# Two layer norms whose later tiles are split in SBUF and transposed by DMA, with a new order of all jobs

## The chip, the core and the metric

The kernel runs on one core of a Trainium2 chip. The time is the device time of one execution in microseconds; the kernel before took 765.34 us as the median of three runs (764.74 to 767.15). Five engines work side by side, each through its own list of instructions in order: TensorE (PE) for matmuls, VectorE (DVE), ScalarE (ACT), GpSimd (POOL) and SyncE (SP), which here does nothing but issue DMA transfers. Matmuls write to PSUM; ACT and DVE carry the results from there to SBUF.

## The reference

Input `x` has 2048 tokens of 512 features. It is normalised, and the result feeds two branches whose sum is added to `x`. (In the sum of the last line `_A_ref` ends with `@ wo`, and `_B_ref` normalises its input a second time.)

```
xn = _layernorm(x)
# A: attention over N = 4 segments of L = 512 tokens, H = 32 heads of 16, with a memory M, z of earlier segments
logits = einsum("bhqd,bhkd->bhqk", qs, ks) * scale + mask
a_dot  = einsum("bhqk,bhkd->bhqd", softmax(logits), vs)
a_mem  = einsum(phi(qs), M) / (einsum(phi(qs), z) + 1e-6)
o = g * a_mem + (1 - g) * a_dot;   M += phi(ks)^T vs;   z += sum phi(ks)
# B: channel MLP, 512 -> 1792 -> 512
y = _layernorm(xn);   h = gelu(y @ w1 + b1);   mlp = h @ w2 + b2
out = x + o @ wo + mlp
```

## The kernel before

**Tiling.** A token tile is 128 tokens by 512 features. The attention runs in 16 units, one for each of four segments and four groups of eight heads; the MLP runs in 16 units, one for each stretch of 256 tokens and each half of the 1792 hidden features. Matrix products are made of float16 parts: an operand is split in a high part and a low part (value times a scale, minus the high part), and a product is three matmuls (`split3`, line 459). So the normalised tokens have to lie in SBUF with features on the partitions, both parts: `xnT` holds a segment for the attention, `yT` 256 tokens for the MLP. There is one buffer of each, so a new segment may be written only when the last reader of the old one is done.

**The norms.** A token tile is loaded into `xt` (two buffers, line 424), its statistics are made on DVE, and POOL applies scale and shift in place (line 412). Then `ln_tr` makes four 128 by 128 transposes on PE into one PSUM tile (line 444), ACT copies the high part out (447) and DVE the low part (448). Of the first norm ("X") there are 16 tiles, of the second ("Y", which loads `x` anew) another 16.

**The jobs.** The work is cut into some 1400 jobs, sorted into streams. In the text: T(i) is a projection of queries or keys of unit i (12 matmuls of 512 columns, line 459), after which ACT and DVE split the result into `hl`, three DMAs write it to DRAM (`qd`, `kd`) and Tr(i) reads it back as stacked rows (`qst`, `kst`, line 500); V is the same for values; M(i) is the pass for row maxima (scores on PE, line 584; masked maximum on DVE, 591); R(i) transposes the maxima (599), which go through DRAM (`md`) into `qst`; S(i) is the scores again (626) with the exponential on ACT (631) and the causal mask on POOL (640); pv and PV multiply by the values (655); O(i) is the chain that divides by the sums (DVE, ACT and POOL, lines 679 to 691); `out` is the output projection of a token tile (782). In the MLP, D is one hidden tile (12 matmuls of 256 columns), G the GELU, H its split, e three matmuls of the second layer (763).

**The order.** Nothing decides the order while the kernel runs: `ORDER` is a string with one letter for each job, a letter names the stream that gives its next job, and each engine gets its instructions in that order, with semaphores in between. SP's list is in the same order, so a DMA that has to wait holds up all DMAs behind it. PSUM has seven rotating tiles for everything but the second MLP layer.

Of the kernel before, what the change touches and what calls it, by code (L numbers as in the profile page):

```python
# [19 lines left out]
P = 128  # L20
D = 512
KT = D // P
# [4 lines left out]
DH = 16  # L27
GH = 8
# [76 lines left out]


ORDER = (
    "aacavveeacccccvccaccvavwwwaawbwwacexxwwwwdfcbyyycxcwwziybxxwygbyxicyzyhyqqzyqqxyqAzAjjjzucqgzqjujrpjrjAzcjAzjf"
    "srpsjjjzssrbzipsujAxikBrcBpssoAjsBsABjAlAqAssljlquljqljAlsqjjCmAmmmjqhjblsjllsqlljqojlBbrBmmcmmjbakBfBqBqriqnq"
    "rginllhqsallsnugllqojjjmmCmBBmqsBljslljlrrujjjjflssljsarjjmiumimmsCsrssjasrnhsrskCnqasssjlqnjllsaaqlllsqqjjmmm"  # L110
    "umarjqjlslsjlaqljsasljsbljsCjjCbfsmmmmrbjssrnokbCgCssqrqinollqqllilqqljsnsjrjjmmmmqjrlsjlsshljlsjlsqjlsjjjmmmm"
    "rofpjinropnkgnipllltulltlujjsprjjjmmmmosjljsjltblujjslblotjjlsmrmmmsjhnskrnssfsqloqsilulqlollsgqinqqmmmmbollos"
    "sjlsljusljshsljbjmmmuramrjqunjqrnfqjqrsijjsoqnjjsrsssoqjskgsqqslallsssaslilsolrrjqjjjummjmmharjssjlqjarssljlaj"
    "ljrssljqsjlaqksmsmammnoqnssaqslsalblsbofnllioolbgbmmmmbhiqllqqllqjlqjlqjromrmmmjnjrnfppjjjsopjjjspsjorsojnrksb"
    "ightslllitllsqljsosjjjmmmmjtljsuusuljlusslljtljjsrmrmmmnjjqrnqqqjkfssroqrsiqllsnollsgillsquosbmmmmbsslosjllsjs"
    "lsjlsljhrujarjmmmmjnjqrnqfuisqsjssrjjorjqqssonjksgssoasslllsssllqqilrajjqrjjqqjarmmmmjjsarljssrssjljslsalllaqj"
    "sasusmmmmnqjqnqhjskassoanbsofllblolillgbimmmmobollflqljlqljqjjrmmmmrnjjrqqpnbjjjsrspsjjosspjoqnjkigtrsslllpoli"
    "ltljssbjjjmmmmqjlsljssljlssljtjrjtjrlmmjqusjmrmnsrnkfqssllsqouqurqqulolliluusgoqsnmmmmibsllsbssllsjlsjqjlursjm"
    "mmmqrnjrjnfjqqrssjisjjoqssrjjqoqsjsrkgssisrsnqrqllolssqsqljrlsjrjsssjlsjmmjjmmqljqljslljljjqlsjkrummmmssnrnssl"
    "llssslllnossmmmmrllllsllorsrmmmmnsssssnnssssstttt"  # L120
)


# [14 lines left out]
def infini_mixer_kernel(ctx: ExitStack, tc: tile.TileContext, x, wq, wk, wv, wo, beta, w1, b1, w2, b2, out):  # L138
    nc = tc.nc
    V, A, G, T, Q = nc.vector, nc.scalar, nc.gpsimd, nc.tensor, nc.sync  # L140
# [3 lines left out]
    cst = ctx.enter_context(tc.tile_pool(name="cst", bufs=1))  # L144
# [295 lines left out]

    def ln_tr(t, dst, c0):
        p = dense()
        for k in range(KT):
            T.transpose(p[:, P * k:P * k + P], t[:, P * k:P * k + P], ident)  # L444
        p3 = p.rearrange("p (k c) -> p k c", k=KT)
        h = dst[:, :, 0, c0:c0 + P]
        A.activation(h, p3, AF.Copy, scale=1024.0)
        V.scalar_tensor_tensor(dst[:, :, 1, c0:c0 + P], p3, 1024.0, h, op0=OP.mult, op1=OP.subtract)  # L448
# [377 lines left out]
    def e_of(j, a, f):  # L826
# [8 lines left out]
        "Y": lambda *k: ln("Y", *k), "Yt": lambda *k: ln_out("Y", *k), "gate": gates,  # L835
# [39 lines left out]
```

## Time and profile before

| | |
|---|---|
| median of three runs | 765.34 us (764.74 to 767.15) |
| the profiled execution | 765.62 us, span 763.9 us |
| PE busy | 721.7 us, 94% of the span |
| DVE, ACT, POOL busy | 550.1, 528.4, 352.9 us |
| mean granted PE clock | 0.984 of full speed |
| transposes of line 444 on `xt` | 120 matmuls |
| DMA issues on SP's queue | none of them a transpose |

The span runs from the first to the last instruction. Busy times are unions of intervals; matmuls overlap in PE's pipeline, so what a piece of work costs PE is read from the distance between starts. "L444" is line 444 of the kernel before. After an arrow in brackets stands what ended an engine's idle time.

### The profile page before, as it was taken

The numbers are of one execution on the slowest core, as the hardware profiler recorded it, in microseconds if no ns is written. First come the engines' busy times: TensorE is split into PE (matmuls) and PEld (weight loads), VectorE is DVE, ScalarE is ACT, GpSimd is POOL, SyncE is SP. The second block draws the span as 40 slices with busy tenths as digits, with TensorE's granted clock in tenths as the row PEclk, the third lists the DMA queues.
The fourth block names the chain that finished last, engine by engine and source line by source line (L and its number), as shares of the span: only waits on it lengthen the run. The fifth ranks groups of instructions, "written<-read, shape, count | busy, mean of one in ns | idle before, by whom it ended". The sixth has DMA issues, their size and how long they took to land.

```text
span 763.9 us, 14514 instructions
## 1 busy us (share of the span) xinstructions
PE 721.7 (94%) x5189; PEld 377.6 (49%) x5189; DVE 550.1 (72%) x1677; ACT 528.4 (69%) x908; POOL 352.9 (46%) x544
## 2 busy tenths in 40 slices
PE   2689999999999999999999999999999999999987
PEld 1354565455643455555454455455555445455433
DVE  5599878998685846888567684979758574777622
ACT  5887898878785478485783577768585567756960
POOL 4466645754624443453434163536335235345461
PEclk9599999999999999999999999999999999999989
DMA  7975314321203223120311324221240315211101
GB/s 206 300 197 146 91 42 107 83 51 51 63 22 113 75 68 103 44 67 23 106 36 36 99 59 125 37 77 30 55 121 1 92 43 108 59 45 42 17 1 56
DMA packets 54084, 59.16 MB, mean 77 GB/s; under 512 B 5038, under 2 KB 40892, under 8 KB 54012
## 3 DMA queue, kind: packets, MB, share of 16 engines
q1 hardware_dynamic: 51708, 54.04, 24.9%
q0 software_dynamic: 2304, 4.20, 3.6%
q8 instruction: 41, 0.67, 0.4%
q14 instruction: 31, 0.25, 0.1%
HBM read 41.18 MB, written 17.04 MB: 76 GB/s over the span
## 4 chain that ended last, share of the span: by engine, by line
PE 77%; ACT 7%; DVE 6%; DMA 5%; issue 2%; SPq 1%; POOL 1%; DVEq 0%; ACTq 0%; POOLq 0%
PE dense L459 31%; PE eacc L763 17%; PE dense L655 8%; PE dense L782 6%; PE dense L584 5%; PE dense L626 5%; ACT pt L631 2%; PE dense L532 2%; PE dense L540 1%; PE dense L560 1%; PE dense L444 1%; DVE dense L591 1%; DMA qst<-qd 1%; DMA qd<-hl 1%; ACT hT L727 1%
## 5 line engine op out<-in xcount | busy, mean ns | idle before, releaser
L591 DVE CUSTOM_DVE_ANT_0 dense<-dense,mask 128x512 f32<-128x512 f32 (+3 forms) x512 | 241.2, 515 | 21.4 <-PE dense L584 14.0
L631 ACT ACTIVATE pt<-dense,qkcs 128x512 f32<-128x512 f32 (+1 forms) x384 | 205.4, 627 | 32.1 <-PE dense L626 31.8
L763 PE MATMUL eacc<-w2s,hT 128*128 128x512 f16 x672 | 171.0, 382 | 1.0 <-DVE acc L767 1.0
L640 POOL TENSOR_SCALAR_AFFINE_SELECT pt<-pt 128x256 f32<-128x256 f32 x256 | 100.9, 426 | 141.1 <-ACT pt L631 140.5
L459 PE MATMUL dense<-yT,w1s 128*128 128x256 f16 x1344 | 161.4, 273 | 3.8 <-DVE yT L448 3.1
L459 PEld LDWEIGHTS <-w1s 128*128 128x128 f16 x1344 | 127.9, 98 | 37.7 <-issue 18.0
L736 POOL TENSOR_TENSOR hT<-hh,hT 128x512 f16<-128x512 f32 x64 | 68.8, 1074 | 88.6 <-ACT hT L735 88.6
L763 PEld LDWEIGHTS <-hT 128*128 128x128 f16 x672 | 58.7, 98 | 77.3 <-issue 27.2
L655 PE MATMUL dense<-pt,vt 128*32 128x512 f32 (+3 forms) x1024 | 79.9, 441 | 0.2
L591 DVE DVE_READ_ACCUMULATOR2_ANT mc<- 128x1 f32 x512 | 72.2, 141 | 0.0
L584 PE MATMUL dense<-kst,qst 48*128 48x512 f16 (+3 forms) x512 | 63.2, 300 | 5.0 <-DVE phk L492 2.2
L735 ACT ACTIVATE hT<-hh 128x512 f16<-128x512 f32 x64 | 36.6, 572 | 43.1 <-POOL hh L734 42.8
L626 PE MATMUL dense<-qst,kst 50*128 50x512 f16 (+3 forms) x512 | 61.7, 300 | 3.5 <-ACT pt L631 1.4
L734 POOL TENSOR_SCALAR hh<-hT,sc 128x512 f32<-128x512 f32 x64 | 42.7, 667 | 40.7 <-ACT hT L727 38.5
L481 DVE SCALAR_TENSOR_TENSOR hl<-dense,hl 128x512 f16<-128x512 f32 x32 | 22.0, 688 | 52.4 <-ACT phq L480 40.1
L655 PEld LDWEIGHTS dense<-pt,vt 128*32 128x32 f32 x1024 | 32.7, 110 | 46.6 <-issue 32.5
L720 ACT ACTIVATE hT<-dense,b1t,sc 128x256 f32<-128x256 f32 x64 | 36.0, 564 | 20.8 <-PE dense L459 20.1
L459 PE MATMUL dense<-xnT,wks 128*128 128x512 f16 x192 | 46.4, 394 | 0.0
L459 PE MATMUL dense<-xnT,wqs 128*128 128x512 f16 x192 | 45.7, 389 | 0.1
L459 PE MATMUL dense<-wvs,xnT 128*128 128x512 f16 x192 | 43.9, 379 | 0.0
L782 PE MATMUL dense<-wos,oT 128*128 128x512 f16 x192 | 43.7, 380 | 0.0
L626 PEld LDWEIGHTS <-kst 50*128 50x128 f16 x512 | 21.0, 94 | 43.8 <-issue 36.0
(223 smaller groups left out, 951.4 us busy)
## 6 DMA issues: line engine op xcount, KB each, us to landing
xt<-in_A_x_dram SPq DMA_DIRECT2D x30, 256.0 KB
kd<-hl SPq DMA_DIRECT2D x48, 128.0 KB
kst<-kd SPq DMA_DIRECT2D x32, 192.0 KB
qd<-hl SPq DMA_DIRECT2D x48, 128.0 KB
qst<-qd SPq DMA_DIRECT2D x32, 192.0 KB
acc<-in_A_x_dram SPq DMA_DIRECT2D x16, 256.0 KB
acc<-in_B_b_dram POOLq DMA_DIRECT2D x16, 256.0 KB, 4.5
out_dram<-acc SPq DMA_DIRECT2D x16, 256.0 KB
```

What stands on the lines that cost most here:

```text
L459: T.matmul(p, wsl(ws, k, a), xsl(xs, k, b), start=s0 and i == 0, stop=s1 and i == 3 * n - 1)
L584: T.matmul(p[:, o:o + n], stk[i, 0][r, t, P * qb:P * qb + P], stk[i, 1][r, t, :n], start=True, stop=True)
L591: V.tensor_tensor_reduce(p[:, o:o + n], p[:, o:o + n], mask[:, 512 - n:], 1.0, -3e38, OP.add, OP.max, mc[i][:, 4 * b + t, qb:qb + 1])
L626: T.matmul(p[:, o:o + n], stk[i, 1][r, t, P * kb:P * kb + P], stk[i, 0][r, t, P * kb:], start=True, stop=True)
L631: A.activation(e[:, OFF[kbs[0]]:OFF[kbs[0]] + o], p[:, :o], AF.Exp, scale=qkcs[:, 1, i % NG:i % NG + 1])
L640: G.affine_select(v, v, pattern=[[0, 2], [1, P]], compare_op=OP.is_ge, fill=0.0, base=0, channel_multiplier=-1)
L655: T.matmul(p[32 * c:32 * c + 32, P * kb:], vt[s, kb][:, 4 * g + c, 16 * odd:16 * odd + 32], pt[i, 2 * c + odd][:, OFF[kb]:OFF[kb] + LEN[kb ...
L734: G.tensor_scalar(t, hz[:, z, :], col(SHH + j % 2), 0.0, op0=OP.mult, op1=OP.add)
L735: A.activation(hT[:, z, 0, :], t, AF.Copy)
L736: G.tensor_tensor(hT[:, z, 1, :], t, hT[:, z, 0, :], op=OP.subtract)
L763: T.matmul(p, t[:, u, P * a:P * a + P], w2s[:, fo, v, :], start=fi == 0 and n == 0, stop=fi == FH - 1 and n == 2)
L782: T.matmul(p, o[:, u, P * b:P * b + P], wos[:, g, v, :], start=i == 0, stop=i == 3 * NG - 1)
```

## The change

For all tiles but those of the first norm's first segment and the second norm's first 256 tokens (26 of 32 tiles), the high and low parts are made in SBUF before the transposition: ACT writes the high part to a new tile `xh` (for the second tile of a pair: to the upper half of the first tile's buffer), DVE writes the low part over the lower half of the tile itself. A separate job ("Xq", "Yq") then sends both parts through a DMA transpose into `xnT` or `yT`: two DMAs of 128 KB for each tile, 52 in all, on SP's queue. The constant `bd` becomes bfloat16 (0 and 1 only). The string `ORDER` is new as a whole.

```diff
@@ streams
-            norm += [("X", n, b, k) for k in range(3)] * (n > 0) + [("Xt", n, b, k) for k in range(2)]
+            norm += [("X", n, b, k) for k in range(3)] * (n > 0) + [(m, n, b, k) for m in ("Xt", "Xq")[:1 + (n > 0)] for k in range(2)]
     for n in range(2 * NSEG):
-        again += [("Y", n, 0, 0), ("Y", n, 0, 2), ("Yt", n, 0, 0), ("Yt", n, 0, 1)]
+        again += [("Y", n, 0, 0), ("Y", n, 0, 2), ("Yt", n, 0, 0), ("Yt", n, 0, 1)] + [("Yq", n, 0, k) for k in range(2)] * (n > 0)
@@ ORDER
-    "llssslllnossmmmmrllllsllorsrmmmmnsssssnnssssstttt"
+    "sssljsrsssljjssssrjljsslsljjslsjkmmmmnnsslllllslnsommmmllllloslmmmmnnntttt"
@@ infini_mixer_kernel
-    bd = cst.tile([P, GH, DH], F32, name="bd")
+    bd = cst.tile([P, GH, DH], BF, name="bd")
...
-    def ln_out(kind, n, b, k):
+    def ln_to(kind, n, b, k):
+
         if kind == "X":
             if n not in xnT:
                 xnT[n] = sb.tile([P, KT, 2, SEG], F16, name="xnT")
-            ln_tr(lt["X", n, b][k], xnT[n], 256 * b + P * k)
+            return xnT[n], 256 * b + P * k
+        if n not in yT:
+            yT[n] = sb.tile([P, KT, 2, 256], F16, name="yT")
+        return yT[n], P * k
+
+    def ln_out(kind, n, b, k):
+        if n == 0:
+            ln_tr(lt[kind, n, b][k], *ln_to(kind, n, b, k))
         else:
-            if n not in yT:
-                yT[n] = sb.tile([P, KT, 2, 256], F16, name="yT")
-            ln_tr(lt["Y", n, b][k], yT[n], P * k)
+            ln_parts(kind, n, b, k)
+
+    lp = {}
+
+    def ln_parts(kind, n, b, k):
+        ts = lt[kind, n, b]
+        t = ts[k]
+        h = sb.tile([P, D], F16, name="xh") if k == 0 else ts[0].bitcast(F16)[:, D:]
+        l = t.bitcast(F16)[:, :D]
+        A.activation(h, t, AF.Copy, scale=1024.0)
+        V.scalar_tensor_tensor(l, t, 1024.0, h, op0=OP.mult, op1=OP.subtract)
+        lp[kind, n, b, k] = h, l
+
+    def ln_send(kind, n, b, k):
+        dst, c0 = ln_to(kind, n, b, k)
+        for a, r in enumerate(lp[kind, n, b, k]):
+            Q.dma_start(dst[:, :, a, c0:c0 + P], r, transpose=True)
```

The order moves much. Two places matter for the text. The first is SP's list around the last pair of tiles of the third segment (`xnT` is about to be read by T of unit 8). In the kernel before:

```order
L604 DMA md_101<-mhl 32x2x128
L609 DMA qst_93<-md_101 2x2048 x2
L424 DMA xt<-in_A_x_dram 128x512 x2
L482 DMA kd_96<-hl 8x16x512
L483 DMA kd_96<-hl 8x16x512
L484 DMA kd_96<-hl 8x16x512
L500 DMA kst_94<-kd_96 48x4x512 x2
```

and in the changed one:

```order
L628 DMA md_101<-mhl 32x2x128
L633 DMA qst_93<-md_101 2x2048 x2
L463 DMA_TRANSPOSE xnT<-xh 128x4x128
L463 DMA_TRANSPOSE xnT<-xt 128x4x128 x3
L424 DMA xt<-in_A_x_dram 128x512 x2
L463 DMA_TRANSPOSE yT<-xh 128x4x128
L463 DMA_TRANSPOSE yT<-xt 128x4x128 x3
L506 DMA kd_96<-hl 8x16x512
L507 DMA kd_96<-hl 8x16x512
L508 DMA kd_96<-hl 8x16x512
```

Four transposes of `xnT` now stand ahead of the loads of the second norm's tiles (which reuse the buffers that the transposes read), and four of `yT` ahead of the writes of unit 8's keys.

The second place is the end of DVE's list, where `acc<-eacc` closes a token tile's half of the second MLP layer (seven e jobs on PE come before each) and `mhl<-dense` belongs to R(15), the last transpose of row maxima. Before (R(15)'s row stands five rows above the first):

```order
L517 SCALAR_TENSOR_TENSOR oT<-oT,nD 128x512
L767 SCALAR_TENSOR_TENSOR acc<-eacc,sc,acc 128x512
L516 TENSOR_TENSOR rc<-rc,ame 128x512
L517 SCALAR_TENSOR_TENSOR rc<-rc,ame 128x512
L541 SCALAR_TENSOR_TENSOR ame<-dense,bg,rc 128x512
L668 SCALAR_TENSOR_TENSOR nN<-dense,bg,nN 128x512
L669 SCALAR_TENSOR_TENSOR nD<-dense,eo,nD 128x512
L679 STREAM_SHUFFLE oT<-nD 128x512
L767 SCALAR_TENSOR_TENSOR acc<-eacc,sc,acc 128x512
L516 TENSOR_TENSOR oT<-oT,nD 128x512
L517 SCALAR_TENSOR_TENSOR oT<-oT,nD 128x512
L767 SCALAR_TENSOR_TENSOR acc<-eacc,sc,acc 128x512
```

Changed (R(15)'s row again five rows above the first):

```order
L541 SCALAR_TENSOR_TENSOR oT<-oT,nD 128x512
L540 TENSOR_TENSOR rc<-rc,ame 128x512
L541 SCALAR_TENSOR_TENSOR rc<-rc,ame 128x512
L565 SCALAR_TENSOR_TENSOR ame<-dense,bg,rc 128x512
L791 SCALAR_TENSOR_TENSOR acc<-eacc,sc,acc 128x512
L692 SCALAR_TENSOR_TENSOR nN<-dense,bg,nN 128x512
L693 SCALAR_TENSOR_TENSOR nD<-dense,eo,nD 128x512
L703 STREAM_SHUFFLE oT<-nD 128x512
L540 TENSOR_TENSOR oT<-oT,nD 128x512
L541 SCALAR_TENSOR_TENSOR oT<-oT,nD 128x512
```

Behind R(15) stood the ends of three halves, and now stands one; the other two, and most of the third's e jobs, come ahead of R(15).

More of the change, by code (lines that the diff above doesn't have):

```diff
@@ L107 @@
 ORDER = (
[L108 to L117, printed above, removed]
@@ L118 @@
-    "ltljssbjjjmmmmqjlsljssljlssljtjrjtjrlmmjqusjmrmnsrnkfqssllsqouqurqqulolliluusgoqsnmmmmibsllsbssllsjlsjqjlursjm"
-    "mmmqrnjrjnfjqqrssjisjjoqssrjjqoqsjsrkgssisrsnqrqllolssqsqljrlsjrjsssjlsjmmjjmmqljqljslljljjqlsjkrummmmssnrnssl"
-    "llssslllnossmmmmrllllsllorsrmmmmnsssssnnssssstttt"
+    "aacaaccvcvaccccccvvvawwwabawewwaexwwxwdwcbfxcyyyxbywwxcczgybhyyxyxxyyizqqqyqqzqicAzcjjgzqzjurjepjczjzzrjjfrpAj"
+    "jzcAiAspuBrjbjpiAsBjsrswBBsAkCssoBsAjAAqsulAjbsllsqjlqljqbljjsAbAmmmmcuhqjlBqlljsqjblobjlsjljBfmjkBmmmBarqqing"
@@ new lines @@
+    "rqlnlliqqualrngllqsjhCBjjmmBmmsrsjlsljlsjlrCBjojjflslqsujjjrmammarmsshiqijrarunCakqsssssqrjuanllnsqalalssssqaj"
+    "llssqajajmamambCmqjllssjljsllbjsrssjrsjjjgrolbmjCbbsbkmrssmomrfsssCsiCillnnllssqqlqbqnlbjjommmmjqljqlljsqjllss"
+    "ljohsjjmmmrmjjfprjpnjnkbgnpbplllistlltiljqjjmrmmmjjrtuljqsljlousjljtluljssjhjmrmmmusjknonfqqsllsoislnssslllsou"
+    "qgmimmmqlluqlsllsboblorajjjmhrmmmnrrjjqnqssjqqsjjjssrsjofqjijsooqqjksgnsqqliallssqslllrsausqjjjqarmjmmmrjarjss"
+    "hrjassljjssausaljlsjsjlaslsljkssmmmmnaaqaanalllqbolblsonblbbbfmmmmoolllgllqbqhlqqimrmrmmnqijjnopjjfqpjrrjpjjjs"
@@ new lines @@
+    "opnsjjjrssqoosjskgtsbilliltosullltsjjjmmrmmqsrjljrsssljlusqljltjljsmmurmmnrjjjsusuuqnhbsqqjkfbqonssqllblbsoaol"
+    "sillgsimrmmmqsroaslrllsussqssljrssjjlqqjljsmrmmmsnsjqnhsjjujsfoqaqrssjjjorqsasrsojngkisorqsaiqssaqrqalllsssqjl"
+    "jslaslqrrsssmmajjmsmsrjljrssjslslajjsljlsjlajaaarmmmmjbknsnbhsssssllssolfbllolbnobbgmimmmbiolllfllqqljqjjmmmmq"
+    "ijbnjppnnjjjpjjopjjqqojkqgtblqlulloitlulrquqjjfjjmmrrmmjrtsljjsssrlljussjlsljjtjlsmimmbmsjnnqqkssqqblsosllblso"
+    "uollngmmmmiqllqllflqjlqrjuqjjrmrmmmnrjrjssnjqsisqrjsssjjjosrssqrujssssojqkgrqqlsrslllnissqqllqrurosjjssmmmmjjr"
@@ L121 @@
+    "sssjljsrsssljjssssrjljsslsljjslsjkmmmmnnsslllllslnsommmmllllloslmmmmnnntttt"
 )
@@ L834, in infini_mixer_kernel @@
         "X": lambda *k: ln("X", *k), "Xt": lambda *k: ln_out("X", *k),
-        "Y": lambda *k: ln("Y", *k), "Yt": lambda *k: ln_out("Y", *k), "gate": gates,
+        "Y": lambda *k: ln("Y", *k), "Yt": lambda *k: ln_out("Y", *k), "Yq": lambda *k: ln_send("Y", *k), "Xq": lambda *k: ln_send("X", *k), "gate": gates,
         "D": lambda j, f: once("D", j, lambda: d_jobs(j))[f](),
```

## The prediction

> **What bounds the kernel now.** I read the page's busy shares, the two strips and the chain first.
>
> ```profile
> span 763.9 us, 14514 instructions
> PE 721.7 (94%) x5189; PEld 377.6 (49%) x5189; DVE 550.1 (72%) x1677; ACT 528.4 (69%) x908; POOL 352.9 (46%) x544
> PE   2689999999999999999999999999999999999987
> PEclk9599999999999999999999999999999999999989
> PE 77%; ACT 7%; DVE 6%; DMA 5%; issue 2%; SPq 1%; POOL 1%; DVEq 0%; ACTq 0%; POOLq 0%
> ```
>
> TensorE (PE) carries 77% of the chain and is full from the third slice to the last two. A busy PE is not a PE at its peak, so I count its work by distances between starts. Then the busy time in three stretches (columns: stretch, its length, PE, PEld, DVE, ACT, POOL, clock, DMA share, GB/s):
>
> ```profile
> 0.00:60.00 60.00, 33.81 (x191) 21.91 (x193) 42.92 (x138) 43.71 (x76) 30.14 (x43) 0.86 0.80 233
> 60.00:714.00 654.00, 644.90 (x4758) 338.66 (x4752) 490.41 (x1515) 458.43 (x789) 301.08 (x468) 1.00 0.26 67
> 714.00:764.00 50.00, 42.98 (x246) 17.05 (x244) 16.78 (x26) 26.29 (x46) 21.66 (x33) 0.93 0.09 28
> 730.00:740.00 10.00, 8.31 (x34) 2.39 (x36) 2.31 (x3) 8.50 (x16) 5.25 (x11) 0.71 0.00 0
> ```
>
> So PE waits 26.2 us in the first 60 us (loads and splits of the weights; the DMA share is 0.80), only 9.1 us in the next 654, and 7.0 us in the last 50, where the clock sags to 0.71 for one stretch. In the middle, a microsecond taken off PE is worth a microsecond. At the two ends it is not.
>
> **The change part by part.** *Transposes off PE.* 26 tiles (12 of the first norm, 14 of the second) lose four transposes each. What one tile holds PE for is the distance from its first transpose to the next work's first matmul, in the timeline of PE:
>
> ```profile
> 103.89 0.64 PE L444 MATMUL dense<-ident,xt 128*128 128x128 f32 x4
> 104.45 2.36 PE L655 MATMUL dense<-pt,vt 128*32 128x512 f32 x32
> ...
> 542.37 0.81 PE L763 MATMUL eacc<-w2s,hT 128*128 128x512 f16 x3
> 543.01 0.60 PE L444 MATMUL dense<-ident,xt 128*128 128x128 f32 x4
> 543.45 1.46 PE L763 MATMUL eacc<-w2s,hT 128*128 128x512 f16 x6
> ```
>
> 0.56 us in the first, 0.44 us in the second; I take 0.49, near their middle: 26 × 0.49 = 12.7 us (11.4 to 14.6). The Trainium skill, "TensorE: Matmul & The Clock Gate", Part 4: PE-mode transpose, puts one such transpose at about 275 ns in a kernel; 104 of them would be an estimated 28.6 us. The recorded length (0.60 us for four overlapped ones) is no cost, and the distance between starts, 0.11 to 0.14 us each, decides.
>
> *ACT and DVE.* Each tile still costs one ACT copy and one DVE subtraction, now reading SBUF. The nearest rows are the weight splits of the same form, beside the present ones:
>
> ```profile
> L366 ACT ACTIVATE w2s<-w2s x7: 613/629/631, 51.9 to 128.6; 128x512 f16<-128x512 f32 x7
> L447 ACT ACTIVATE xnT<-dense x16: 577/597/632, 12.3 to 545.4; 128x512 f16<-128x512 f32 x16
> L363 DVE SCALAR_TENSOR_TENSOR w2s<-w2s,sc x5: 746/1090/1192, 54.5 to 115.1; 128x512 f16<-128x512 f32 x5
> L448 DVE SCALAR_TENSOR_TENSOR xnT<-dense,xnT x16: 677/690/692, 13.1 to 546.1; 128x512 f16<-128x512 f32 x16
> ```
>
> That is +0.03 us on ACT and +0.06 to +0.40 us on DVE per tile: at most 26 × 0.40 = 10.4 us of DVE, covered by the 163.6 us it has free in the middle stretch (654 − 490.4). I count nothing; uncovered it would be those 10.4 us. A new wait comes with it: the second tile's high part is written over the upper half of the first tile, so ACT waits there for DVE's first subtraction, with the exponentials of S queued behind; ACT's 195 us free in that stretch hide it. The mask `bd` in bfloat16 touches 20 small DVE instructions; nothing either way.
>
> *DMA transposes.* 52 of them, 128 KB each, all on SP's queue. The trace has no such operation. The nearest row is a plain 128 KB DMA (`kd`, `qd`), whose landing is what the next issue waits for:
>
> ```profile
> 142.84 0.68 SPq L484 DMA_DIRECT2D kd<-hl  x1
> 147.56 0.80 SPq L500 DMA_DIRECT2D kst<-kd  x2
> ...
> 193.68 0.58 SPq L484 DMA_DIRECT2D qd<-hl  x1
> ...
> 196.69 0.79 SPq L500 DMA_DIRECT2D qst<-qd  x2
> ```
>
> From issue to landing 3.0 to 4.7 us, 0.63 us of issue each; a group of four (two tiles, two parts) lands 3 × 0.63 + 3.0..4.7 = 4.9 to 6.6 us after it may start. For the upper bound I use the page's packets:
>
> ```profile
> DMA packets 54084, 59.16 MB, mean 77 GB/s; under 512 B 5038, under 2 KB 40892, under 8 KB 54012
> q1 hardware_dynamic: 51708, 54.04, 24.9%
> ```
>
> 0.249 × 16 × 763.9 us / 51708 = 59 ns per packet of about 1 KB. If a transpose goes in pieces of 256 B at that price, it has 512 and holds the 16 engines 1.9 us; the group lands after 4 × 1.9 + 3 = 10.6 us. I take the plain DMA's figure, the only row of the same size. Cover, from the changed order of PE's work at the distances of this trace (2.6 us a projection of 12 matmuls, 1.36 us a D job, 0.70 us an e job, 0.24 to 0.35 us an M or S job, 0.58 us a pv job): between the last reader of the old `yT` and the first of the new stand 8.3, 24.3, 7.4, 13.3, 10.6, 38.4 and 10.6 us for the seven later halves; only the third (7.4) is near 6.6. For `xnT` the last pair has 10.6, 4.6 and 10.3 us from its place to the first projection. The middle one is short: its splits take 0.63 + 0.75 + 0.63 + 0.75 = 2.8 us, then 3.0 to 4.7 us to land, so PE waits 1.2 to 2.9 us. I add **2.0 us** for waits. SP is in order, so at that place the `x` loads stand behind the transposes (their tiles are the sources), then four transposes of `yT`, then the `kd` writes of the next keys; M of unit 8, which reads them, has 20.7 us of PE work ahead of it. The row maxima `md` of other units stand behind such loads too; before, they also stood behind loads that waited for PE, so I count no loss.
>
> *The order at the end.* This is the part that speaks against the gain. R(15), the last row-maximum transpose, starts at 714.45 us. Its tail in PE's timeline, and the last head chain on DVE and POOL:
>
> ```profile
> 714.45 0.27 PE L599 MATMUL dense<-ident,mc 128*32 128x128 f32 x1
> 714.65 2.36 PE L655 MATMUL dense<-pt,vt 128*32 128x512 f32 x32
> 716.94 2.76 PE L763 MATMUL eacc<-w2s,hT 128*128 128x512 f16 x12
> ...
> 738.46 3.59 PE L655 MATMUL dense<-pt,vt 128*32 128x512 f32 x32
> 741.98 2.12 PE L763 MATMUL eacc<-w2s,hT 128*128 128x512 f16 x9
> 745.05 4.69 PE L763 MATMUL eacc<-w2s,hT 128*128 128x512 f16 x21 [0.95 <-DVE acc L767]
> 749.58 10.52 PE L782 MATMUL dense<-wos,oT 128*128 128x512 f16 x48
> 742.19 0.75 DVE L668 SCALAR_TENSOR_TENSOR nN<-dense,bg,nN 128x512 f32<-128x512 f32 x1 [4.10 <-PE dense L655]
> 750.57 1.15 POOL L691 TENSOR_TENSOR oT<-nN,oT 128x512 f16<-128x512 f32 x1 [0.74 <-ACT oT L690]
> 720.55 0.61 ACT L735 ACTIVATE hT<-hh 128x512 f16<-128x512 f32 x1
> 721.07 6.18 ACT L631 ACTIVATE pt<-dense,qkcs 128x512 f32<-128x512 f32 x12
> 731.97 6.20 ACT L631 ACTIVATE pt<-dense,qkcs 128x512 f32<-128x512 f32 x12
> ```
>
> Behind R(15) before stand 21 e jobs (63 matmuls L763); in the change 5. The e jobs fill PE while ACT makes two times twelve exponentials (6.2 us each, with the head chain between) and while the last head chain runs from 742.19 to 751.72 us. Those chains set the tail's length with or without filler, so taking 16 e jobs out of it shortens nothing: the tail stays 763.9 − 714.45 = 49.5 us. ACT loses the `hT` splits that stand right before each set of exponentials (0.61 us the one at 720.55), at most 1.2 us: I take −0.9. But the 16 jobs, 48 matmuls at 0.223 us (4.69 / 21), now stand ahead of R(15), in the full stretch: **+10.7 us**. And with PE idle for some 7 us of that 9.5 us head chain, the 39 matmuls of the output that wait for it begin at a low clock: here are twelve 512-column matmuls in the cold start and in the middle:
>
> ```profile
> 22.84 5.10 PE L459 MATMUL dense<-xnT,wks 128*128 128x512 f16 x12
> 107.30 2.75 PE L459 MATMUL dense<-xnT,wks 128*128 128x512 f16 x12
> ```
>
> 0.2 us more each; for about ten of them +1.9 us (0 if the clock holds, 4 if it returns late).
>
> *Waits that go.* The order has 48 fewer places where PE changes from one kind of job to another (682 to 634, counted over both orders). By the rows above a switch costs nothing (an e job alone holds PE 0.64 us, from 542.37 to 543.01, one of seven in a row 4.69 / 7 = 0.67) up to 0.12 us (the two distances of the transposed tiles): 0 to −5.8, and I take 0.04 us each, −2.0 us. Of the 9.1 us that PE waits between 60 and 714 us I let the moved jobs fill half, −4.5 us (bounds 0 and −9.1): D of units 13 to 15 stand 14 to 20 us of PE work earlier, so their GELU is long done when an e job is wanted. The start keeps its loads and its squares; ±2 us, taken as 0.
>
> Sum against the profiled execution (765.62 us, its span 763.9 and 1.7 around it, 0.3 us above the median of 765.34): 765.6 − 12.7 + 10.7 − 0.9 + 1.9 + 2.0 − 2.0 − 4.5 = **760.1 us**, the forecast; its own range is 755.5 (all 9.1 us of waits filled) to 764.6 (none).
>
> **Rivals.** *A: the moved e jobs cost nothing.* Then nearly all 12.7 us are kept: 765.6 − 12.7 + 2.0 − 0.9 = 754.0, with the clock held. For it: DVE's maxima of one unit take (241.2 + 72.2) / 16 = 19.6 us, and the moved jobs stand among those of unit 15, where PE may wait for DVE. Against it: PE waits only 9.1 us in 654.
>
> ```profile
> L591 DVE CUSTOM_DVE_ANT_0 dense<-dense,mask 128x512 f32<-128x512 f32 (+3 forms) x512 | 241.2, 515 | 21.4 <-PE dense L584 14.0 <-PE dense L626 1.4 <-ACT pt L631 1.0
> L591 DVE DVE_READ_ACCUMULATOR2_ANT mc<- 128x1 f32 x512 | 72.2, 141 | 0.0
> ```
>
> *B (slower): the transposes land late and PE stands before D and T.* It decides from a group's landing of 7.4 us on. At 10.6 us the seven `yT` waits are 2.3 + 0 + 3.2 + 0 + 0 + 0 + 0 us, and the three of `xnT` about 2.8 + 8.8 + 3.1 (splits 2.8, landing 10.6, covers as above): 20 us against the 2.0 counted, so 760.1 + 18 = 778. For it: nothing in the trace shows a transposing DMA at a plain one's speed. Against it: SP and the DMA engines are a quarter busy. The Trainium skill, "Advanced Engine Details and Errata", DGE: Hardware vs Software, rates the transpose efficiency of DMAs issued from the sync and scalar queues as worse; the same page's section on the X-bar transpose calls them as fast as plain ones. No run here shows either.
>
> *C: no change.* The order's second-order gains (−6.5) don't come: 765.6 − 12.7 + 10.7 − 0.9 + 1.9 + 2.0 = 766.6. The change would do what it says and the tail would give it back.
>
> **How the numbers follow.** Forecast 0.42, A 0.20, B 0.18, C 0.20. A measurement here tells 0.3% (2.3 us) from no change: below 763.0 is faster, above 767.6 slower. About three quarters of the forecast's own range lie below 763.0 (0.32 faster, 0.10 same); A is faster; B slower; C splits 0.12 same and 0.08 slower. That gives 0.52, 0.22 and 0.26. The range runs from A's sum less the upper price of the transposes (754.0 − 1.9 = 752) to just short of B's sum: 776.
>
> **What would show it.** Right: L444 falls from 120 to 16 matmuls on `xt`, PE's middle stretch stays full, R(15) starts at 708 to 712 us, and from it to the end are 48 to 51 us with PE idle before the last out matmuls. Wrong towards A: R(15) before 706 us. Wrong towards B: PE waits on a DMA of `yT` or `xnT` in the list of waits, over 10 us together. Wrong otherwise: a first D or T several us later than 43 and 23 us, or a tail whose clock or exponentials changed its length.

## The result: slower by 4.7%, and the profile after

The changed kernel takes 800.39 us (median, 798.85 to 804.99) against 765.04 us for the kernel before on the same chip: a ratio of 1.0474 (95% interval 1.0452 to 1.0495). The forecast was 760.1 us, the range 752 to 776; slower was given 0.26. Sign and size were wrong.

The page of the changed kernel, with the lines that answer to those shown of before (line numbers are those of the changed kernel: L444 is now L468, L584 L608, L626 L650, L599 L623, L763 L787, L782 L806):

```profile
span 796.9 us, 14467 instructions
PE 725.3 (91%) x5085; PEld 370.0 (46%) x5085; DVE 546.2 (69%) x1677; ACT 528.3 (66%) x908; POOL 353.8 (44%) x544
PE   2699999998997999997999999999798999999885
PEclk9799999999998999999899999999999999999998
```

PE has 104 transposes fewer and yet is busy longer (725.3 against 721.7 us), and its strip has holes in the middle that were not there. The same in three stretches, cut at R(15):

```profile
0.00:60.00 60.00, 35.74 (x203) 22.22 (x204) 44.53 (x150) 44.69 (x78) 30.07 (x45) 0.89 0.80 239
60.00:749.00 689.00, 656.71 (x4687) 334.73 (x4685) 488.58 (x1507) 464.39 (x794) 310.46 (x478) 0.99 0.30 73
749.00:797.00 48.00, 32.85 (x196) 13.06 (x196) 13.10 (x21) 19.19 (x36) 13.28 (x22) 0.92 0.06 23
```

In the first 60 us PE does 2 us more than before. The middle, 654 us before, is 689 us, and PE waits 32.3 us in it instead of 9.1. The tail is about as long as forecast. In PE's timeline (after, first the R(15) that ends the middle, then the last head chain's output matmuls):

```profile
749.10 0.27 PE L623 MATMUL dense<-ident,mc 128*32 128x128 f32 x1 [0.91 <-DVE mc L615]
...
773.57 2.12 PE L806 MATMUL dense<-wos,oT 128*128 128x512 f16 x9
782.16 1.03 PE L806 MATMUL dense<-wos,oT 128*128 128x512 f16 x2 [6.47 <-ACT oT L714]
```

R(15) starts 34.7 us later than before (749.10 against 714.45); from it to the end are 47.8 us, forecast 48 to 51, with PE idle for 6.5 us ahead of the output. So all of the loss arises ahead of R(15), where the forecast itself put 10.7 us of moved e jobs. Who PE waited for, in the list of PE's waits between 60 us and R(15), first before, then after (us in total, times, longest):

```profile
PE dense L584 <- DMA qst<-qd: 0.6, 1, 0.6
PE dense L626 <- DMA qst<-md: 0.2, 1, 0.2
```

```profile
PE dense L608 <- DMA qst<-qd: 8.7, 5, 4.5
PE dense L650 <- DMA qst<-md: 5.6, 3, 2.8
```

These two are 14.3 of the 32.3 us; the rest is spread over DVE, ACT and POOL, the largest item 2.5 us (`acc`, four times). PE does not wait for a DMA of `yT` or `xnT`, which was to be the sign of rival B, but for the rows of queries and of row maxima that make a round trip through DRAM. Both the writes and the reads of these trips stand in SP's queue, and so do the new transposes. SP's timeline near unit 3, before and after:

```profile
188.21 0.34 SPq L604 DMA_DIRECT2D md<-mhl  x1
189.64 0.55 SPq L609 DMA_DIRECT2D qst<-md  x2
```

```profile
190.30 0.35 SPq L628 DMA_DIRECT2D md<-mhl  x1
190.71 1.22 SPq L463 DMA_TRANSPOSE yT<-xh  x1
191.97 3.99 SPq L463 DMA_TRANSPOSE yT<-xt  x3
196.06 0.68 SPq L633 DMA_DIRECT2D qst<-md  x2
```

From the write of the maxima to their read went 1.4 us before and 5.8 us after, and S(3) waited 2.8 us for it on PE. A transpose holds SP for 1.2 us, where the prediction had 0.63 us from a plain DMA of the same size (a group of line 463, with minimum, median and maximum of an issue in ns):

```profile
L463 SPq DMA_TRANSPOSE yT<-xt x21: 1189/1217/2322, 100.0 to 672.3; - x21
```

Behind some of the waits comes a second price. Eight stretches of the changed kernel, and one at the same place before (after the length, PE's busy time; the granted clock is the third number from the right):

```profile
158.00:168.00 10.00, 8.51 (x64) 4.76 (x65) 7.18 (x31) 5.85 (x12) 6.64 (x12) 1.00 0.29 64
168.30:171.70 3.40, 3.40 (x31) 2.14 (x24) 3.15 (x10) 1.62 (x3) 2.12 (x2) 0.50 0.39 78
188.00:199.00 11.00, 8.16 (x54) 3.53 (x52) 9.67 (x18) 5.33 (x11) 5.73 (x8) 1.00 0.41 84
199.00:202.40 3.40, 3.40 (x9) 1.16 (x9) 0.53 (x1) 3.37 (x7) 0.81 (x2) 0.50 0.25 84
244.00:253.60 9.60, 5.97 (x32) 2.37 (x30) 2.22 (x3) 5.46 (x11) 3.80 (x9) 1.00 0.34 106
253.60:260.40 6.80, 5.67 (x28) 2.52 (x32) 2.58 (x9) 1.08 (x2) 0.59 (x1) 0.50 0.05 10
367.00:376.50 9.50, 7.54 (x69) 3.54 (x69) 7.10 (x29) 4.33 (x9) 3.05 (x6) 1.00 0.02 4
376.50:383.30 6.80, 5.87 (x23) 2.86 (x22) 3.81 (x7) 6.29 (x12) 3.45 (x5) 0.50 0.42 80
```

```profile
253.60:260.40 6.80, 6.80 (x39) 2.70 (x37) 5.68 (x21) 4.41 (x8) 1.82 (x5) 1.00 0.34 117
```

After a stretch in which PE was busy for 62 to 85% of the time, it runs at half clock for 3.4 or 6.8 us. These four are all that the middle has after, 20.4 us together, which is up to 10.2 us of lost work; before, the clock stays at 1.00 from 60 to 714 us. The Trainium skill, "TensorE: Matmul & The Clock Gate", Part 1: The HAM clock gate, puts the half rate, in its table of the two states, behind at least one idle window of some 3.4 us. Half clock in steps of 3.4 us is what the trace shows. An idle time that long stands ahead of only one of the four stretches, the third (PE's wait of 4.5 us ends at 254.5 us); ahead of the other three the longest single waits were 1.1, 2.8 and 1.7 us.

### The profile page after: what moved, and what is told of

The parts are those of the page before. It is cut to its first block, busy times and chain, and to the rows that moved or that the text cites. A ratio compares the mean times of both kernels' runs of the same rounds, so it can differ in the third digit from the quotient of the medians.

```text
span 796.9 us, 14467 instructions
## 1 busy us (share of the span) xinstructions
PE 725.3 (91%) x5085; PEld 370.0 (46%) x5085; DVE 546.2 (69%) x1677; ACT 528.3 (66%) x908; POOL 353.8 (44%) x544
## 2 busy tenths in 40 slices
DMA packets 82372, 65.97 MB, mean 83 GB/s; under 512 B 33326, under 2 KB 69180, under 8 KB 82300
## 3 DMA queue, kind: packets, MB, share of 16 engines
q1 hardware_dynamic: 79996, 60.86, 28.8%
## 4 chain that ended last, share of the span: by engine, by line
PE 38%; DVE 5%; DMA 4%; ACT 3%; POOL 1%; issue 1%; SPq 0%; POOLq 0%; DVEq 0%; ACTq 0%
PE dense L483 15%; PE eacc L787 8%; PE dense L679 4%; PE dense L806 4%; PE dense L608 2%; PE dense L650 2%; DVE dense L615 2%; DMA qst<-qd 1%; ACT pt L655 1%; PE dense L564 1%; DMA xt<-in_A_x_dram 1%; PE dense L556 1%; DMA qd<-hl 1%; DMA xnT<-xt 1%; PE dense L584 1%
## 5 line engine op out<-in xcount | busy, mean ns | idle before, releaser
L787 PE MATMUL eacc<-w2s,hT 128*128 128x512 f16 x672 | 171.2, 384 | 3.9 <-DVE acc L791 2.5
L483 PE MATMUL dense<-yT,w1s 128*128 128x256 f16 x1344 | 164.6, 276 | 3.5 <-DVE yT L472 1.2
L483 PEld LDWEIGHTS <-w1s 128*128 128x128 f16 x1344 | 129.4, 99 | 38.5 <-issue 12.7
L760 POOL TENSOR_TENSOR hT<-hh,hT 128x512 f16<-128x512 f32 x64 | 67.0, 1046 | 84.2 <-ACT hT L759 83.4
L787 PEld LDWEIGHTS <-hT 128*128 128x128 f16 x672 | 58.5, 98 | 81.3 <-issue 27.5
L679 PE MATMUL dense<-pt,vt 128*32 128x512 f32 (+3 forms) x1024 | 84.7, 444 | 1.5 <-POOL pt L664 1.1
L608 PE MATMUL dense<-kst,qst 48*128 48x512 f16 (+3 forms) x512 | 62.7, 302 | 14.0 <-DMA qst<-qd 8.7
L650 PE MATMUL dense<-qst,kst 50*128 50x512 f16 (+3 forms) x512 | 62.1, 302 | 11.4 <-DMA qst<-md 6.5
L806 PE MATMUL dense<-wos,oT 128*128 128x512 f16 x192 | 45.8, 390 | 6.7 <-ACT oT L714 6.5
L709 POOL TENSOR_TENSOR nN<-nN,oT 128x512 f32<-128x512 f32 x16 | 21.0, 1312 | 68.2 <-DVE oT L541 68.2
L650 PEld LDWEIGHTS <-kst 50*128 50x128 f16 x512 | 21.5, 94 | 54.7 <-issue 45.6
L608 PEld LDWEIGHTS <-qst 48*128 48x128 f16 x512 | 21.7, 94 | 52.6 <-issue 33.9
```

The source lines that it names most:

```text
L483: T.matmul(p, wsl(ws, k, a), xsl(xs, k, b), start=s0 and i == 0, stop=s1 and i == 3 * n - 1)
L608: T.matmul(p[:, o:o + n], stk[i, 0][r, t, P * qb:P * qb + P], stk[i, 1][r, t, :n], start=True, stop=True)
L650: T.matmul(p[:, o:o + n], stk[i, 1][r, t, P * kb:P * kb + P], stk[i, 0][r, t, P * kb:], start=True, stop=True)
L679: T.matmul(p[32 * c:32 * c + 32, P * kb:], vt[s, kb][:, 4 * g + c, 16 * odd:16 * odd + 32], pt[i, 2 * c + odd][:, OFF[kb]:OFF[kb] + LEN[kb ...
L760: G.tensor_tensor(hT[:, z, 1, :], t, hT[:, z, 0, :], op=OP.subtract)
L787: T.matmul(p, t[:, u, P * a:P * a + P], w2s[:, fo, v, :], start=fi == 0 and n == 0, stop=fi == FH - 1 and n == 2)
```

## The experiments

The first theory, **Q**: SP's in-order queue, held by transposes of 1.2 us each, makes the round trips late, and that is the loss. The first rival, **O**: the new order is slower by itself, whoever transposes. A third, **S**: the splits in SBUF, where ACT and DVE wait for each other.

### Who loses: the order, the splits or the transposes

**The transposes left out.**

```diff
     def ln_send(kind, n, b, k):
-        dst, c0 = ln_to(kind, n, b, k)
-        for a, r in enumerate(lp[kind, n, b, k]):
-            Q.dma_start(dst[:, :, a, c0:c0 + P], r, transpose=True)
+        return
```

> The new order with the splits left in and the 52 DMA transposes left out; later tokens read the first tiles' xnT and yT again, so the output is not the reference's. Theory Q (the transposes hold SP's in-order queue, 1.22 us each, and what stands behind them - row maxima, query and key rows, loads of x - comes late): the 35 us lost ahead of the last row-maximum transpose go, 755 to 770 us. Rival O (the new order is bad by itself, whoever transposes): 790 to 800. Rival S (the splits on ACT and DVE, which wait for each other, are what stalls): 785 to 800 as well, told from O by the run with the transposes on TensorE.

Measured: 786.2 us, ratio to before 1.029 (1.0263 to 1.0317), above Q's range and below O's. The transposes cost 14.2 us, but most of the loss stays without them.

**TensorE transposes in the new order.**

```diff
     def ln_send(kind, n, b, k):
-        dst, c0 = ln_to(kind, n, b, k)
-        for a, r in enumerate(lp[kind, n, b, k]):
-            Q.dma_start(dst[:, :, a, c0:c0 + P], r, transpose=True)
+        ln_tr(lt[kind, n, b][k], *ln_to(kind, n, b, k))
```

> The new order with the transposes back on TensorE, at the places where the DMA transposes were issued; no splits in SBUF. Theory Q: about the time before plus or minus 10 us, 760 to 778 (12.7 us of TensorE come back, the 35 us of late data go). Rival O: 800 to 812 (the loss stays and 12 us of TensorE come on top). Rival S: as Q.

Measured: 800.8 us, ratio 1.048 (1.0446 to 1.0513): as O said. The new order loses 36 us with the old transposes. From this run to the one without transposes are 14.6 us: that is what 104 transposes take of PE, less what the 26 splits cost. The forecast for the transposes alone was 12.7, so nothing is left for the splits, and S falls. So the DMA transposes cost as much as they saved.

**The old order with DMA transposes.**

```diff
-    ORDER, streams: those of the changed kernel
+    ORDER, streams: those of before; each Xt, Yt makes the parts and sends them at once
```

> The order before, with the same splits and the 52 DMA transposes at the places where TensorE transposed. Theory Q: slower than before, 780 to 830, since the same 52 x 1.22 us stand in SP's queue and the first readers follow sooner after the transposes than in the new order. Rival O: faster than before, 750 to 760.

Measured: 806.5 us, ratio 1.0534 (1.0498 to 1.0571). Here rival B's sign is there, in the list of PE's waits:

```profile
PE dense L484 <- DMA yT<-xt: 18.5, 9, 4.1
PE dense L484 <- DMA xnT<-xt: 5.4, 4, 2.6
```

In the old order the readers follow too soon. The new order does give the transposes room; it pays for that elsewhere.

**Plain copies in place of transposes.**

```diff
-            Q.dma_start(dst[:, :, a, c0:c0 + P], r, transpose=True)
+            Q.dma_start(dst[:, :, a, c0:c0 + P], r.rearrange("p (k c) -> p k c", k=KT))
```

> The new order with each DMA transpose replaced by a plain DMA of the same 128 KB from the same tile to the same tile, rows of 256 bytes, not transposed (so the output is not the reference's). Theory Q with the length of the issue as the cause: 0.6 us of SP each instead of 1.22, some 32 us less in that queue, about half of the loss returns, 775 to 785. If it is the landing or the chain of waits (a load behind the transposes that read its tile) and not the length of the issue: 790 to 800.

Measured: 790.8 us, ratio 1.0341 (1.0319 to 1.0364). The issue:

```profile
L463 SPq DMA_DIRECT2D yT<-xt x21: 594/617/659, 100.8 to 660.7; - x21
```

The time lies in the range of the rival (landing, or the chain of waits), but Q's range gave the queue half of the whole loss, and 786.2 us is all that can come back here. Measured from there, an issue of 0.6 us in place of 1.2 for the same bytes takes the cost of the 52 DMAs from 14.2 to 4.6 us. A later landing could do that too, but the traces speak against it: in seven places the two loads of `x` that reuse the tiles follow a group at once in SP's queue, and both are out 1.6 to 4.2 us after SP is done with the group's last transpose, and 2.1 to 4.2 us after its last plain copy. So a transpose is later by its issue and not by its data.

### What the new order loses: moving jobs

In the run without transposes two places stand out. At one, the read of unit 5's query rows stands behind an output store in SP's queue that waits for DVE, and PE waits 4.2 us for the rows (4.5 us in the changed kernel); at the other, the trip of the maxima of unit 7 has too little work ahead of it (SP, then PE, of the run without transposes):

```profile
241.57 3.59 SPq L725 DMA_DIRECT2D out_dram<-acc  x2
245.33 0.84 SPq L523 DMA_DIRECT2D qst<-qd  x2
```

```profile
362.67 0.28 PE L622 MATMUL dense<-ident,mc 128*32 128x128 f32 x1
369.81 0.90 PE L649 MATMUL dense<-qst,kst 50*128 50x512 f16 x8 [1.85 <-DMA qst<-md]
```

The trip of the maxima takes 7.1 us here. Counted over both orders at the distances of the trace of before, 6.8 us of PE work stand on average between R(i) and S(i) in the new one and 7.7 in the old, and less in 12 of 16 units; at unit 7 4.9 against 10.2.

**Two jobs moved.**

```diff
-    ... V  S4 S4 S4  Tr(5, keys)  E out  S4 S4 out  Tr(5, queries)  S4 M5 ...
+    ... V  Tr(5, keys) Tr(5, queries)  S4 S4 S4  E out  S4 S4 out  S4 M5 ...
```

> The new order with TensorE's transposes, and two jobs moved: the reads of the key and query rows of unit 5 are issued ahead of the output store that stands in SP's queue before them. Theory: the 4.4 us for which TensorE waits for qst<-qd near 250 us, the 2.4 us around it and the 3.4 us that the half clock behind it costs go: 791 to 795 from 800.8. Rival (the wait is only handed on to the next late thing): 799 to 802.

Measured: 794.3 us, ratio 1.0386 (1.0368 to 1.0405): 6.5 us from two letters, as expected: more than the wait of 4.4 us that went, since the half clock behind it went too.

**All trips early, and more work between R and S.**

```diff
-    each Tr(i), Rr(i) where the new order has it
+    each Tr(i) behind T(i), each Rr(i) behind R(i), as far as the buffers allow;
+    e, D and M jobs from behind S(i) pulled ahead of it until 8.5 us stand there
```

> The new order with TensorE's transposes; all reads of key and query rows and of row maxima are issued as early as their data and buffers allow, and up to 3 us of jobs of MLP and row maxima are pulled between the last row-maximum transpose R(i) of a unit and its first S job, so that 8.5 us of TensorE work (against 4.4 to 8.0) stand there, but for units 7, 11 and 15. Theory (the 23 us that the new order loses are round trips that it covers too little): 780 to 788. Rival (many small things, or an engine that is short over stretches of 10 us and more): 795 to 800.

> The changed kernel with the early reads and with 8.5 us of work between R(i) and the first S job of a unit, as in the run with TensorE's transposes. Theory: 775 to 785. Rival: 795 to 800.

Measured: 846.6 us, ratio 1.1052 (1.1006 to 1.1097), with TensorE's transposes, and 844.4 us, ratio 1.1052 (1.1021 to 1.1084), with DMA. Both wrong by far. PE's waits in the first:

```profile
PE dense L606 <- DMA qst<-qd: 19.0, 10, 5.1
```

In the run that it started from this was 5.9 us: M jobs that were pulled ahead now come before their own query rows have landed. Between 60 us and R(15) the clock is at half for some 61 us, against 10 there, up to 31 us of lost work. **The early reads alone**, in the changed kernel:

> The changed kernel with all reads of key and query rows and of row maxima issued as early as their data and buffers allow, so that three of them stand ahead of a group of DMA transposes in SP's queue and not behind it. Theory (SP's in-order queue makes the reads late, by stores and by the 1.22 us of each transpose): 786 to 792 from 800.4. Rival (the queue is not what is late): 798 to 802.

Measured: 808.3 us, ratio 1.058 (1.0537 to 1.0622), 8 us slower than the change and outside both ranges. A read that is issued early may wait at the head of SP's queue for its data, and everything behind it with it; that this is what cost the 8 us was not shown. These three runs say little on the cause; they show how stiff the order is.

**Three jobs moved in the changed kernel.**

```diff
-    ... R3 ..  Yq(2) Yq(2)  Rr(3) ...       and Tr(5) as above
+    ... R3  Rr(3)  ..  Yq(2) Yq(2) ...
```

> The changed kernel with three of its 1,360 jobs moved: the reads of unit 5's key and query rows ahead of the output store before them in SP's queue, and the read of unit 3's row maxima ahead of four DMA transposes. Theory: 6.5 us as in the run with TensorE's transposes, and 3 us of waits and 1.7 us of half clock near 195 us: 787 to 791. Rival (each wait is only handed on): 796 to 801.

Measured: 795.2 us, ratio 1.0401 (1.0378 to 1.0425), 5.2 us less instead of 9 to 13. Unit 5's wait went, and S(3)'s. But unit 4's query rows, which come behind the same transposes, were next:

```profile
207.47 0.39 PE L608 MATMUL dense<-kst,qst 48*128 48x512 f16 x1 [2.60 <-DMA qst<-qd]
```

### The round trips taken away

The two theories can be taken apart without moving anything, by leaving the trips out.

```diff
-        Q.dma_start(d[:, rows[0]:rows[0] + 16, :], hl[:, 0, :])
+        for j, h in enumerate((0, 0, 1)) if i < 2 else ():
+            Q.dma_start(d[:, rows[j]:rows[j] + 16, :], hl[:, h, :])
...
-        for b in range(2):
+        for b in range(2 * (i < 2)):
             Q.dma_start(t[i % 2][64 * b:64 * b + 48], ...)
```

The same goes for `md`.

> The kernel before with the round trips through DRAM left out from unit 2 on: no write of query and key rows or row maxima to DRAM and no read of them back (M and S of the later units read the rows of units 0 and 1 again, so the output is not the reference's). It says what the trips cost the order before. Theory (the order before covers them): 756 to 763. Rival (they cost both orders alike): below 750.

> The new order with TensorE's transposes and, as in the run beside it, without the round trips from unit 2 on. Theory (what the new order loses ahead of the last row-maximum transpose, 25 us, is mostly these trips and the half clock behind their waits): 775 to 782, so that it stands 14 to 22 us above the order before without trips (10 us of it the tail). Rival (other engines' waits, that is, PSUM buffers and VectorE's row maxima): 790 to 798.

> The changed kernel without the round trips from unit 2 on. Theory (the 14 us that the DMA transposes cost are the trips' DMAs that stand behind them in SP's queue): 762 to 770, some 12 us below the run with TensorE's transposes, which is what the 104 transposes take of TensorE. Rival (the transposes land late by themselves): about equal to it, 775 to 790.

> The new order with the splits, without the DMA transposes and without the round trips from unit 2 on (later tokens read the first xnT and yT again and later units the first rows, so the output is not the reference's). With the trips in, leaving out the transposes was worth 14.2 us (800.4 to 786.2). If all of that are trips held up behind transposes, then without trips it is worth next to nothing: 775 to 777, as the changed kernel without trips (777.0). Rival (the transposes are late for TensorE by themselves too): 765 to 772.

Medians in us, with the ratios to before (765.0):

| | all work | no trips | ratio without trips |
|---|---|---|---|
| old order, transposes on TensorE | 765.0 | 764.4 | 0.9986 (0.9970 to 1.0001) |
| new order, transposes on TensorE | 800.8 | 790.8 | 1.0336 (1.0317 to 1.0355) |
| new order, DMA transposes (the change) | 800.4 | 777.0 | 1.0161 (1.0138 to 1.0184) |
| new order, no transposes | 786.2 | 777.4 | 1.0166 (1.0144 to 1.0188) |

Each ratio is to the kernel before in the same batch; by the ratios the differences below change by at most 1.0 us. The old order covers its trips entirely. In the new one they cost 10.0 us even with TensorE's transposes, less than the 19 to 26 expected (790.8 lies in the range of that run's rival: other engines' waits), and 23.4 us with the DMA transposes. Without trips the DMA transposes cost nothing (777.0 against 777.4), and taking 104 transposes off PE is worth 13.8 us (790.8 to 777.0), all that was forecast. So the 14 us that the DMA transposes cost are, to within the measurement, trips that stand behind them; theory Q holds for this part and no more. (777.0 lies in the rival's range, transposes that land late by themselves, but only because the run with TensorE's transposes came out higher than that range assumed: the distance of some 12 us that the theory named is 13.8.)

### What is left: the norms, the tail

Without trips the new order is still 26.4 us behind the old (790.8 to 764.4).

```diff
     def ln(kind, n, b, part):
+        if n > 0:
+            return
```

`ln_out` and `ln_send` do likewise.

> The kernel before, without the round trips from unit 2 on, and without the norms of all later tokens too: no load of x, statistics, normalising, transposes or splits behind the first segment and the first two halves (the first xnT and yT are read again; the output is not the reference's). With the run beside it, it says whether what the new order still loses without the trips (26 us, 10 of them in the tail) lies in the chain of the later tokens' norms. 764.4 less 12.7 us of transposes: 750 to 753.

> The new order without the trips and without the norms of later tokens, as the run beside it. Theory N (the new order squeezes the chain load of x, statistics, normalising, split of a segment into a few us): it stands 10 to 14 us above the old order cut in the same way, 760 to 766. Rival (row maxima, exponentials and MLP jobs themselves stand worse): 20 to 26 us above it, 771 to 778.

Measured: 748.8 us (ratio 0.9782, 0.9769 to 0.9795) and 766.4 us (1.0013, 1.0001 to 1.0024), 17.6 us apart, between the two theories' figures. So 8.8 of the 26.4 us come with the later tokens' norms. The new order without trips, in which they were measured, shows part of how, in the list of PE's waits between 60 us and R(15), in PE's timeline and in a stretch behind it:

```profile
PE dense L648 <- DVE xnT L470: 1.8, 1, 1.8
PE dense L466 <- DVE xnT L470: 1.2, 1, 1.2
PE dense L605 <- DVE yT L470: 0.8, 1, 0.8
PE dense L466 <- POOL xt L412: 0.5, 1, 0.5
```

```profile
373.97 0.27 PE L648 MATMUL dense<-qst,kst 50*128 50x256 f16 x1 [1.84 <-DVE xnT L470]
```

```profile
374.40:377.60 3.20, 3.20 (x18) 1.77 (x17) 2.25 (x4) 2.95 (x7) 2.19 (x2) 0.51 0.00 0
```

PE waits 4.5 us in all (with a last wait of 0.2 for `yT`) for steps of the transposition and the split (S, which reads no `xnT`, presumably for the PSUM tile that DVE still reads), 0.9 us in the old order without trips. That is 3.6 of the 8.8 us; the rest was not taken apart. Behind the longest of these waits the clock halves for 3.4 us, but it does so once in the old order without trips too (136.6 to 140 us), so the half clock makes no difference here. Of the remaining 17.6 us the tail explains most. R(15) in PE's timeline, old order and new, both without trips and norms:

```profile
699.02 0.27 PE L602 MATMUL dense<-ident,mc 128*32 128x128 f32 x1
```

```profile
716.42 0.27 PE L626 MATMUL dense<-ident,mc 128*32 128x128 f32 x1 [0.91 <-DVE mc L618]
```

17.4 us apart, with 48.7 (747.7 − 699.0) and 49.0 us (765.4 − 716.4) behind it. 16 e jobs have gone from behind R(15) to ahead of it, by the prediction's price 10.7 of the 17.4 us, and the tail did not get shorter. Some 7 us are left. Between 60 us and R(15) PE is busy for 13.5 us longer than in the old order (644.1 against 630.6), 2.8 more than that price, and idle for 3.9 us longer (12.3 against 8.4), in no single wait above 1.7 us; the clock is full in both. This was not taken apart further.

### Could the gain be had?

**Another queue.**

```diff
-            Q.dma_start(dst[:, :, a, c0:c0 + P], r, transpose=True)
+            A.dma_start(dst[:, :, a, c0:c0 + P], r, transpose=True)
```

> The changed kernel with all 52 DMA transposes issued from ScalarE's queue and not from SP's. Theory: SP's queue is clear, so the 13 us of held-up trips come back, but each issue holds ScalarE for some 1.2 us, 63 us in groups of four, ahead of the exponentials of S: 785 to 800. Rival (ScalarE's exponentials are as urgent as the trips): 801 to 815.

Measured: 837.9 us, far outside both. An issue takes 1.2 us there too, and PE now waits for ACT:

```profile
PE dense L650 <- ACT nD L688: 11.5, 4, 4.1
PE dense L650 <- ACT pt L655: 8.2, 14, 3.1
```

**The old order, with DMA only where there is room.**

```diff
-            ln_tr(lt["X", n, b][k], xnT[n], 256 * b + P * k)
+        if n == 0 or kind == "Y" or b == 1:
+            ln_tr(lt[kind, n, b][k], *ln_to(kind, n, b, k))
+        else:
+            ln_parts(kind, n, b, k)
+            ln_send(kind, n, b, k)
```

> The order before with DMA transposes for six tiles alone, the first pair of the first norm in segments 1 to 3, behind which 21 to 30 us of TensorE work stand before the first reader; all others stay on TensorE. Six tiles at 0.49 us: 2.9 us less, 761 to 763, if nothing but a late load of the next pair comes with it. Rival (the next load of x waits for the transposes and its splits come late, with the half clock behind it): 767 to 775.

Measured: 764.8 us, ratio 0.9995 (0.9978 to 1.0011): no change, and neither range. Six tiles' 2.9 us were forecast, but near 155 us S(2) waits for its maxima, and the clock halves behind it (PE's timeline, and the stretch):

```profile
155.84 0.77 PE L651 MATMUL dense<-qst,kst 50*128 50x512 f16 x2 [1.64 <-DMA qst<-md]
```

```profile
155.60:159.00 3.40, 3.16 (x14) 1.75 (x14) 0.79 (x4) 1.78 (x3) 1.25 (x2) 0.50 0.49 92
```

With the pair of half 5 of the second norm on DMA too, and the read of those maxima ahead of the transposes:

```diff
-    ... R2  Xt(1,0,0) ..  Rr(2) ...            if n == 0 or kind == "Y" or b == 1:
+    ... R2  Rr(2)  Xt(1,0,0) ..  ...           if n == 0 or kind == "Y" and n != 5 or b == 1:
```

> The order before with DMA transposes for eight tiles (the first pair of the first norm in segments 1 to 3 and the pair of the second norm's half 5, behind which 11 us of work stand), and the read of unit 2's row maxima moved ahead of the transposes that held it up by 2 us and dropped the clock for 3.4 us in the run with six tiles. 8 tiles at 0.49 us less what loads come late: 760 to 762. Rival (another read behind the transposes is late next): 764 to 767.

Measured: 765.8 us, ratio 1.0006 (0.9993 to 1.0019): the rival. SP's timeline at the place, before and in this run, and then PE's:

```profile
150.35 0.44 SPq L604 DMA_DIRECT2D md<-mhl  x1
155.06 0.53 SPq L609 DMA_DIRECT2D qst<-md  x2
```

```profile
150.28 0.30 SPq L629 DMA_DIRECT2D md<-mhl  x1
155.88 0.53 SPq L634 DMA_DIRECT2D qst<-md  x2
```

```profile
157.51 0.56 PE L651 MATMUL dense<-qst,kst 50*128 50x512 f16 x2 [1.39 <-DMA qst<-md]
```

The transposes are behind the read now and S(2) waits all the same. They had not held the read up: in the run with six tiles SP stood idle from 152.2 to 154.2 us ahead of it, until the write of the maxima, issued at 148.3 us, had landed. The write lands late in all three kernels, 4.7 us after its issue before and 5.6 us in the last run; why is not known. Before, two transposed tiles (0.9 us of PE work by the distances between starts) stood between R(2) and S(2) and helped to hide that; off PE, they leave a hole of their own size. No version found here beats the kernel before.

## Why the prediction was wrong, step by step

- **What bounds the kernel** (a microsecond off PE is worth a microsecond in the middle): right only where what runs beside PE has room. Without trips the transposes were worth 13.8 us, about the 12.7 of the sum. With them, nothing.
- **ACT and DVE at nothing**: right. The splits read SBUF as fast as they read PSUM before, and with them but without any transposes the new order is 14.6 us faster than with TensorE's transposes and no splits, where 12.7 us were counted for the transposes alone. The groups of lines 456 and 457, with minimum, median and maximum in ns:

```profile
L456 ACT ACTIVATE xh<-xt x13: 612/622/644, 88.0 to 628.6; 128x512 f16<-128x512 f32 x13
```

```profile
L457 DVE SCALAR_TENSOR_TENSOR xt<-xt,xh x13: 677/686/993, 88.8 to 631.2; 128x512 f16<-128x512 f32 x13
```

- **DMA transposes, +2.0 us**: the step that failed first; 14.2 us measured. The issue was taken as 0.63 us, from a plain DMA, and is 1.22. A group's landing was about right (forecast up to 6.6 us; from 376.22, the first issue of a group, to 383.22, where its transposes have landed in the chain of waits, it is 7.0 us with splits in between), and PE had the cover for it. The cost was where the text said "I count no loss": the row maxima and key and query rows behind the transposes in SP's queue. The covers were computed for `xnT` and `yT` and not for the trips that pass the same queue. The landing in the chain of waits (start, length):

```profile
380.80 2.42 DMA xnT<-xt
```

- **The order at the end, +10.7, −0.9, +1.9**: right to within a few us. R(15) to the end was 47.8 us, 1.7 us less than before where 1.0 more was counted, and in the two kernels without trips and norms the tails are alike and R(15) comes 17.4 us later, which has room for the 10.7; the 10.7 was not measured by itself.
- **Waits that go, −2.0 and −4.5**: the step that failed most. With TensorE's transposes the new order is 36 us slower; these steps and those of the tail gave it +5.2 (10.7 − 0.9 + 1.9 − 2.0 − 4.5). The 48 fewer switches and the filled waits did not show. In their place came 10.0 us for trips, 8.8 that go with the later norms and some 7 that stay unexplained. Part of the first is the half clock: between 60 us and R(15) it lasts 10.2 us in the new order with TensorE's transposes and 3.4 us without trips, so up to 3.4 of the 10.0 us. The working took the waits of the old order as given and asked which of them go; it did not ask which new ones a wholly new order makes.
- **Rivals**: A and C fall with the same step. B named the right side and the right parts (the transposes, slower than a plain DMA), but the wrong waiter: PE does not stand before D and T, it stands before M and S.

## What to carry to other kernels

When a change puts DMAs into an in-order queue, work out the cover of everything else that passes that queue, and above all of write-then-read trips through DRAM; the data that the new DMAs carry may be the least urgent there. A kernel whose order is written out by hand owes its full PE to some dozens of covers, here of some 5 to 11 us between R and S: cost a new order cover by cover, trip for trip, and take work that is removed out of the covers in which it stood. A wait in a stretch that was full can cost more than itself: to take away one of 4.4 us brought 6.5 us here.

## What the hardware showed that was not expected

- A DMA transpose of 128 KB within SBUF holds the issuing queue for 1.22 us, a plain DMA of the same tile and target 0.62 us; on ACT's queue it is 1.21 to 1.29 us.
- The packets rise from 54,084 to 82,372, 544 for each of the 52 transposes, all of them under 512 B; 512 would be pieces of 256 B, and what the other 32 are the runs do not show. The DMA engines' share in the queue rises only from 24.9 to 28.8% of the span: by these shares an estimated 22 ns for each added packet, so the bound worked out from 59 ns a packet was far too high.
- Half clock in the middle of a full kernel, for 3.4 or 6.8 us, behind stretches of about 10 us in which PE was busy for 62 to 85%. There is more of it in the kernels in which PE waits more: between 60 us and R(15) none before, 20 us after, some 44 us in the old order with DMA transposes and some 61 us with all trips early. No threshold can be read from it: the run with eight tiles has 3.4 us of it from 350.7 us on, where PE had waited for 1.3 us in the ten before (0.33, 0.47 and 0.49 us):

```profile
350.70:354.10 3.40, 3.40 (x13) 0.93 (x12) 2.65 (x12) 2.00 (x5) 2.40 (x6) 0.50 0.44 111
```

The cause was not tested by itself.
